# Products and operand sums in another order, slabs in pairs, and weight sums one stage sooner in a chunk attention, Fourier mixing and MLP kernel on Trainium2

## The chip, the cores and the metric

The kernel runs on one core of one Trainium2 chip. The metric is the time of one execution on the device in microseconds; the kernel before took 1138.69 us (median of three runs, 1135.14 to 1141.55). A profile of one further execution is at hand for the kernel before. Engine names in the profile: PE is TensorE (PEld its weight loads), DVE is VectorE, ACT is ScalarE, POOL is GpSimd, SP is SyncE, which issues most DMAs.

## What is computed

Eight batches of 576 tokens, 8 heads of 64 elements. Attention runs inside chunks of 64 tokens; its output x (576 x 512 per batch) is mixed by the real part of a two-dimensional Fourier transform, then a normalised MLP with a hidden width of 2048 is added. Everything is float32.

```python
scores = scale * np.matmul(q_c, k_c.transpose(0, 1, 2, 4, 3))     # per chunk of 64 tokens
attn = softmax(scores); x = np.matmul(attn, v_c)                  # then (B, S, H*D)
mixed = np.real(np.fft.fft(np.fft.fft(x, axis=1), axis=2))
u = x + mixed
un = (u - mean(u)) / np.sqrt(var(u) + 1e-06)
out = u + np.maximum(un @ w_ch1, 0.0) @ w_ch2                     # w_ch1 512x2048, w_ch2 2048x512
```

The weights arrive as float64 and are rounded to float32 in the kernel.

## The kernel before

*Tiles and stages.* A tile is 128 tokens. A stage of the MLP handles a group of four tiles (512 tokens); there are nine stages: one for each batch and a last one for the four tiles of left-over tokens. Within a group the tiles are LO, HI, LO, HI: an HI tile holds its features reversed. Each stage has an up half (un @ w_ch1, with ReLU, into the hidden tile `h1`) and a down half (`h1` @ w_ch2, plus u, stored to DRAM). While TensorE works on stage g, the attention and the mixing of batch g + 1 are woven in between the MLP's steps: the main loop takes one step of `mlp(g)`, then as many steps of `side(b)` (attention, then `fourier`) as are due, then the work on the weights. The instructions of each engine, SP's DMA queue included, run in the order in which this loop writes them (`manual_schedule`); waits between engines are set by the buffers that they share. SP issues the loads of q, k and v (`load`, `load_v`, L236 and L259), the stores of the result (`store`, L1013 and L1022, some of them on ACT) and the slabs of weights.

*Stages 0 and 1* are plain products with both weights resident in SBUF: `wa` holds w_ch1 (four rows k of 2048 columns), `wb` holds w_ch2 (sixteen rows m of 512). `up_first`, `up_plain` (L1130) and `down_plain` (L1147) take 16 steps for each half, so that stage 1 runs from t = 32 (`begin[1]`) to t = 64 (`begin[2]`).

*Stages 2 to 8* use fewer products on half-size blocks. `up_halves` takes seven products where a plain two by two split has eight: each product is four matmuls (two row blocks r, two kk) of 128x128 by 128x256, and the sums that it needs are taken by VectorE (L1199, L1201, L1203, L1207, L1210) and ACT. `down_halves` takes 26 products of four matmuls each (L1238): `h1` is seen as 4 x 4 blocks a_ij (tile i, quarter j of the hidden width), w_ch2 as 4 x 2 blocks b_ij. `PRODUCTS` lists, for each product, the left operand (an a block or one of the sums y0 to y3 in `yall`), the right operand (a b block or a made sum s..), the half bank of PSUM that it goes to (four banks; a capital letter is the upper half), and the output blocks that it is added to. A half bank that comes again is not cleared: the new product is added to what stands there. VectorE adds or subtracts a half bank to the output (L1248), which must be done before TensorE writes to that half bank again. The a blocks are overwritten in place by POOL's operand sums (`SUMS`, L1098): those named "early" during the up half, the others after the product whose name they carry.

*Weights for these stages.* During stage 1, `keep1` makes the four sums of w_ch1's blocks on POOL (into `yall`) and stores seven slabs for each of four groups to DRAM (`s1`); it has five steps a group. `keep_raw` stores the raw blocks of w_ch2, and `keep_made` makes their 23 sums (`MADE`, L1066: every third on POOL, the others on VectorE), in slots that lie in `wa` and `yall`, and stores the 18 that are needed (`s2`). In the loop, two steps of `keep1` and one raw block are done at each t from `begin[1]` on; the sums, two at each t, begin after `begin[1] + KF` (t = 49); when the last is made (t = 60), ten slabs of `s1` are fetched; at t = 64 six slabs of `s2`.

*Slabs.* In stages 2 to 8, `fetch(1)` brings the next slab of 256 KB of `s1` into one of ten slots in `wa` after each up product (L1078), and `fetch(2)` the next slab of 512 KB of `s2` into one of six slots in `wb` after each down product (L1081). A fetch waits until TensorE is done with the slab that it overwrites.

*Mixing* ends, for each of two LO, HI pairs of tiles, with two VectorE operations on the products (L834, L835), the sum x + mixed for the LO tile on VectorE and for the HI tile on POOL (both L841), and the statistics of both on VectorE (L688, L689). It falls into the first products of a down half.

The lines of the kernel before, as the profile names them:

Of the kernel before, what the change touches and what calls it, by code (L numbers as in the profile page):

```python
# [16 lines left out]
def kernel(  # L17
# [87 lines left out]
    s1 = dram.tile([HF // 2, NO, 128, 2 * 2 * 128], FP32, name="s1")  # L105
    NS1, NS2, Z1, Z2 = 10, 6, 2 * 2 * 128, 4 * HM
    slab1 = [wa[:, i * Z1:(i + 1) * Z1].rearrange("p (k r f) -> p k r f", r=2, k=2) for i in range(NS1)]
    slab2 = [wb[:, i * Z2:(i + 1) * Z2].rearrange("p (m e) -> p m e", m=4) for i in range(NS2)]
# [6 lines left out]
        ("2", "a41", "b11", "c", "+41"), ("13", "a44", "b42", "b", "+42"), ("8", "y0", "s8", "d", "+12"),  # L115
        ("21", "y3", "s21", "c", "+31+32+42"), ("0", "y1", "s0", "d", "+11+21"), ("16", "a22", "b22", "f", "-22"),
        ("19", "a23", "s19", "d", "+22"), ("15", "a44", "s15", "b", "+41"), ("10", "a31", "s10", "f", "+32"),
        ("3", "y1", "s3", "b", "-21-22"), ("11", "y3", "b32", "f", "+42"), ("5", "a22", "b21", "C", "+31"),
        ("24", "a21", "s24", "B", "-32-42"), ("1", "a31", "s1", "D", "-21+41"), ("17", "a13", "s17", "F", "+11"),
        ("4", "a24", "s4", "C", "-21"), ("22", "a41", "s22", "B", "-21"), ("25", "a32", "s25", "D", "-32"),  # L120
        ("12", "a34", "s12", "F", "+12"), ("20", "a43", "b31", "C", "+41"), ("7", "a11", "s7", "B", ""),
        ("6", "a14", "s6", "D", ""), ("18", "y2", "s18", "F", "-32"), ("9", "a12", "b21", "B", "-11"),
        ("14", "y0", "b22", "D", "+12"), ("23", "a33", "s23", "F", "-31"),
    )
    SUMS = {
        "early": "y0=a11-a13 a11=a11-a21 y1=y0-a21 y2=a31-a41 a31=a33-a31 y3=y2-a33",
        "": "a24=a23+a24", "2": "a41=a22+a42 a22=a21-a22 a21=a41-a21", "13": "a44=a24+a44 a31=a21+a31",
        "21": "y3=y3+a43", "0": "y1=a44-y1 y1=y1-a23 y0=a12-y0", "16": "a22=a32-a34 a32=a42-a32",
        "10": "a31=a42-a22 a13=a13+a14 a24=a24+a31 a14=a14+a34 a34=a13+a34 y2=a34+y2",
        "11": "a43=a44+a43 a12=a41-a12 a12=a12+a13 y0=y0-a32",  # L130
    }
    RAW = ("b11", "b42", "b22", "b32", "b21", "b31")
    MADE = (
        "u=b41-b31 0", "s15=u-b42 1", "s7=u-b11 2", "s8=b12+b22 3", "s0=u-s8 4", "t=b32-b42 5", "s19=u+t 5",
        "s3=b31-b41 6", "s10=b11-b12 0", "s21=s10-b32 1", "s24=s10-b22 2", "v=b32-b31 3", "s23=v-s10 3",
        "w=b22-b21 4", "s22=w-s10 5", "s4=b42-b41 6", "s25=w+s4 4", "s1=b21-s4 2", "s17=b21+b41 0",
        "h=b12+b32 1", "s12=h-s17 3", "s6=b42-h 5", "s18=-h 1",
    )
    SLABS = RAW + tuple(name.split("=")[0] for name in MADE if name[0] == "s")
    NR2 = len(PRODUCTS)  # L140
    s2 = dram.tile([len(SLABS), 128, Z2], FP32, name="s2")
# [39 lines left out]
    def kind(n):  # L181
        return tiles[n][0]
# [595 lines left out]
    def fourier(b):  # L778
# [59 lines left out]
        def added(y, n):  # L838
            x, w = xt(n), DM + (kind(n) == HI)
            eng = nc.gpsimd if kind(n) == HI else nc.vector  # L840
            eng.tensor_tensor(out=x[:, 0:w], in0=y[:, 0:w], in1=x[:, 0:w], op=ALU.add)  # L841
# [183 lines left out]
    def keep1(i):  # L1025
# [11 lines left out]
        to = s1.rearrange("a o p (k x) -> p a o k x", k=2)[:, 2 * f:2 * f + 2]  # L1037
        for o, a in enumerate((a11, o2, o1, o3, a12, o4, a22)):
            nc.sync.dma_start(out=to[:, :, o, kk], in_=a.rearrange("p (a x) -> p a x", a=2))
# [6 lines left out]

    def keep_raw(name):
        to = s2[SLABS.index(name)].rearrange("p (m e) -> p m e", m=4)
        nc.sync.dma_start(out=to, in_=block_b(name))

    at_slot = {}

    def keep_made(i):

        text, slot = MADE[i].split()
        space = wa[:, 0:5 * Z2] if int(slot) < 5 else yall.rearrange("p a b -> p (a b)")
        j = int(slot) % 5
        to = space[:, j * Z2:(j + 1) * Z2].rearrange("p (m e) -> p m e", m=4)
        if "=-" in text:
            name, a = text.split("=-")  # L1060
            nc.vector.tensor_scalar(to, at_slot[a], -1.0, None, ALU.mult)
        else:
            name, a, b, op = parsed(text)
            eng = nc.gpsimd if i % 3 == 2 else nc.vector
            in0, in1 = (block_b(x) if x[0] == "b" else at_slot[x] for x in (a, b))
            eng.tensor_tensor(out=to, in0=in0, in1=in1, op=op)  # L1066
        at_slot[name] = to
        if name in SLABS:
            nc.sync.dma_start(out=s2[SLABS.index(name)], in_=to.rearrange("p m e -> p (m e)"))

# [3 lines left out]
    def fetch(which):  # L1074
        i = n_slab[which]
        if which == 1 and i < HF // 2 * NO * (NG - first_of[1]):
            pair, o = divmod(i % (HF // 2 * NO), NO)
            nc.sync.dma_start(out=slab1[i % NS1].rearrange("p k r f -> p (k r f)"), in_=s1[pair, UP[o]])  # L1078
        elif which == 2 and i < NR2 * (NG - first_of[2]):
            slab = SLABS.index(PRODUCTS[i % NR2][2])  # L1080
            nc.sync.dma_start(out=slab2[i % NS2].rearrange("p m e -> p (m e)"), in_=s2[slab])  # L1081
        n_slab[which] = i + 1
# [93 lines left out]
    def up_halves(g):  # L1176
# [3 lines left out]
        for pair in range(HF // 2):  # L1180
            pas, pbs = {}, {}
            for turn_, o in enumerate(UP):
                w = slab1[((g - first_of[1]) * HF // 2 * NO + pair * NO + turn_) % NS1]
# [28 lines left out]
                fetch(1)  # L1212
                if pair == HF // 4 and turn_ > 0:
                    sums(h1, SUMS["early"].split()[turn_ - 1:turn_])
                if turn_ in (1, 3, 5, 6):
                    yield h1

    def down_halves(g, h1):
        banks, begun = {}, set()
        left = [sum(p[4].count(f"{i + 1}{j + 1}") for p in PRODUCTS for j in range(2)) for i in range(G)]  # L1220
        sums(h1, SUMS[""].split())
        for o, (name, a, _, bank, reads) in enumerate(PRODUCTS):
            w, lhs = slab2[((g - first_of[2]) * NR2 + o) % NS2], block_a(h1, a)
# [28 lines left out]
            sums(h1, SUMS.get(name, "").split())  # L1252
            fetch(2)
            if o % 2 == 0:
                continue
            if g + 1 < NG:
                for j in range(G):
                    if k == 3 + 2 * j:
                        normed(g + 1, j)
                    if k == 5 + 2 * j and j >= 2:  # L1260
                        combined(g + 1, j - 2)
# [8 lines left out]
    with tc.manual_schedule():  # L1270
# [73 lines left out]
        for g in range(NG):  # L1344
            for _ in mlp(g):
# [23 lines left out]
                if t >= begin[1]:  # L1369
                    for _ in range(2):  # L1370
                        next(conv1, None)
# [3 lines left out]
                if t > begin[1] + KF and n_made < len(MADE):  # L1375
                    for _ in range(2):
                        if n_made < len(MADE):
                            keep_made(n_made)
                            n_made += 1
                    if n_made == len(MADE):  # L1380
                        for _ in range(NS1):
                            fetch(1)
                if t == begin[2]:
# [51 lines left out]
```

## Time and profile before

| | |
|---|---|
| runs | 1138.69 us median (1135.14, 1138.69, 1141.55) |
| profiled execution | 1134.59 us, span 1132.7 us from its first instruction to its last |
| granted TensorE clock | 0.977 mean |
| HBM | 203.5 MB read, 29.4 MB written, 206 GB/s over the span |
| SP's DMA queue | 163372 packets, 229.54 MB |
| slabs of `s2` (wb<-s) | 182 DMAs of 512 KB |
| slabs of `s1` (wa<-s) | 196 DMAs of 256 KB |
| start of stages 1, 2 and 3 on TensorE | 190, 318 and 450 us |
| start of stages 4 to 8 | 573, 700, 824, 940 and 1036 us |

How to read it: times in the timeline count from the span's start. A line such as `657.00 1.97 PE L1238 MATMUL dn<-wb,yall ... x8 [0.79 <-issue]` says when a run of instructions began, how long it lasted, the engine, the source line, what it writes and reads, how many there were, and in brackets how long the engine had been idle before and what ended that wait. A matmul in float32 appears as two rows, so that one product of four matmuls is eight rows. The waits view adds the same brackets up: who waited for whom, microseconds in total, how often, the longest.

### The profile page before, as it was taken

The page shows a single profiled execution, that of the slowest core. Times are in us where ns is not written, and L with a number is a line of the kernel's source. Part 1 is how long each engine was busy: PE and PEld are TensorE (multiplying, and loading weights), DVE is VectorE, ACT ScalarE, POOL GpSimd, SP SyncE. Part 2 cuts the span into 40 slices and gives each one's busy share as a digit, 9 for nine tenths or more (in the row PEclk, how much of TensorE's full clock was granted, in tenths as well). Part 3 has the DMA queues.
Part 4 walks back from the last instruction along what each step waited for, and adds up shares of the span by engine and source line. Part 5 has one row for each costly group of instructions (what it writes and reads, how often), then busy time and mean ns, then how long its engine had stood idle before and what let it go on. Part 6 is the DMA issues. An engine that isn't in the chain of part 4 may idle for free.

```text
span 1132.7 us, 19622 instructions
## 1 busy us (share of the span) xinstructions
PE 1061.9 (94%) x7210; PEld 812.1 (72%) x7210; DVE 585.1 (52%) x1275; ACT 306.5 (27%) x716; POOL 440.0 (39%) x518
## 2 busy tenths in 40 slices
PE   8999989999996989799989989898989999999998
PEld 6645444444565877687878877687878788888886
DVE  4899873235854355454545465444653543333332
ACT  4697553211121310232122311222022302201210
POOL 4311011365414580076406560078325640380272
PEclk9999999999998999999998999999999999999999
DMA  7767512885468868796778668876865676587456
GB/s 167 233 194 203 139 43 64 287 257 197 184 178 258 251 199 273 199 242 198 228 219 227 206 211 249 221 201 195 271 230 141 195 244 224 161 286 262 125 200 209
DMA packets 167117, 234.20 MB, mean 207 GB/s; under 512 B 70092, under 2 KB 106956, under 8 KB 167022
## 3 DMA queue, kind: packets, MB, share of 16 engines
q1 hardware_dynamic: 163372, 229.54, 66.7%
q10 hardware_dynamic: 3330, 2.76, 0.9%
q8 instruction: 58, 0.95, 0.4%
q0 software_dynamic: 320, 0.66, 0.2%
q14 instruction: 37, 0.30, 0.1%
HBM read 203.53 MB, written 29.36 MB: 206 GB/s over the span
## 4 chain that ended last, share of the span: by engine, by line
PE 70%; DMA 10%; DVE 7%; POOL 4%; ACT 3%; SPq 3%; issue 2%; POOLq 0%; DVEq 0%; ACTq 0%
PE dn L1238 24%; PE pa L1193 15%; PE pb L1193 11%; PE dn L1147 6%; PE up L1130 5%; DMA wb<-s 3%; PE pt L383 2%; DMA k<-in_k_dram 2%; POOL xall L841 2%; DMA xall<-in_moe_w_ch_dram 2%; PE z L705 1%; SPq L249 1%; PE xp L484 1%; PE sc L434 1%; POOL h L1098 1%
## 5 line engine op out<-in xcount | busy, mean ns | idle before, releaser
L1238 PE MATMUL dn<-wb,h 128*128 128x256 f32 x1064 | 240.9, 380 | 0.7 <-DMA wb<-s 0.7
L1238 PEld LDWEIGHTS dn<-wb,h 128*128 128x128 f32 x1064 | 198.9, 190 | 26.6 <-DVE wb L1248 1.1
L1098 POOL TENSOR_TENSOR h<-h 128x512 f32<-128x512 f32 x126 | 161.2, 1293 | 91.0 <-ACT h L1211 70.2
L1193 PE MATMUL pa<-unT,wa 128*128 128x256 f32 x672 | 163.2, 386 | 9.2 <-DVE wa L1201 9.2
L1193 PEld LDWEIGHTS pa<-unT,wa 128*128 128x128 f32 x672 | 127.9, 192 | 28.4 <-DVE wa L1201 10.0
L1248 DVE TENSOR_TENSOR wb<-wb,dn 128x256 f32<-128x256 f32 x154 | 61.6, 417 | 129.5 <-PE dn L1238 129.5
L1238 PE MATMUL dn<-wb,yall 128*128 128x256 f32 x392 | 101.3, 411 | 19.4 <-DVE wb L1248 11.9
L1147 PE MATMUL dn<-wb,h 128*128 128x512 f32 x256 | 114.6, 597 | 0.0
L1193 PE MATMUL pb<-wa 128*128 128x256 f32 x448 | 107.2, 382 | 0.0
L1238 PEld LDWEIGHTS dn<-wb,yall 128*128 128x128 f32 x392 | 78.8, 205 | 35.6 <-DVE wb L1248 13.9
L1193 PEld LDWEIGHTS pb<-wa 128*128 128x128 f32 x448 | 84.6, 191 | 12.4 <-DVE o L1160 0.7
L1147 PEld LDWEIGHTS dn<-wb,h 128*128 128x128 f32 x256 | 46.9, 190 | 51.7 <-issue 50.5
L541 POOL COPY xall<-xall 1x512 f32<-1x512 f32 x28 | 17.8, 635 | 147.0 <-DVE xall L501 119.5
L1193 PE MATMUL pb<-unT,wa 128*128 128x256 f32 x224 | 54.8, 388 | 12.7 <-DMA wa<-s 12.7
L1205 ACT ACTIVATE h<-pa 128x256 f32<-128x256 f32 x56 | 21.5, 384 | 155.3 <-PE pa L1193 155.3
L1210 DVE TENSOR_TENSOR h<-pb,wa 128x256 f32<-128x256 f32 x56 | 23.8, 425 | 73.9 <-PE pb L1193 73.9
L1193 PEld LDWEIGHTS pb<-unT,wa 128*128 128x128 f32 x224 | 43.7, 196 | 20.0 <-issue 13.9
L1130 PE MATMUL up<-unT,wa 128*128 128x512 f32 x128 | 56.6, 595 | 0.0
L1193 PE MATMUL pa<-wa 128*128 128x256 f32 x224 | 56.3, 396 | 0.0
L1199 DVE TENSOR_TENSOR wa<-pb,wa 128x256 f32<-128x256 f32 x56 | 23.4, 423 | 57.3 <-ACT wa L1198 57.3
L1098 POOL TENSOR_TENSOR yall<-h 128x512 f32<-128x512 f32 x14 | 17.8, 1270 | 86.5 <-ACT h L1211 86.2
L512 POOL COPY xall<-xall 128x1 f32<-128x1 f32 x15 | 2.8, 186 | 124.9 <-DVE xall L501 107.7
(258 smaller groups left out, 1602.6 us busy)
## 6 DMA issues: line engine op xcount, KB each, us to landing
wb<-s SPq DMA_DIRECT2D x182, 512.0 KB
wa<-s SPq DMA_DIRECT2D x196, 256.0 KB
xall<-in_moe_w_ch_dram SPq DMA_DIRECT2D x22, 512.0 KB
q<-in_q_dram SPq DMA_DIRECT2D x96, 112.0 KB
k<-in_k_dram SPq DMA_DIRECT2D x96, 112.0 KB
v<-in_v_dram SPq DMA_DIRECT2D x124, 64.0 KB
s<-wa SPq DMA_DIRECT2D x13, 512.0 KB
yall<-in_moe_w_ch_dram SPq DMA_DIRECT2D x10, 512.0 KB
```

Source lines behind the costliest of these rows:

```text
L383: nc.tensor.transpose(pt[:, j, :], src(j), ident)
L541: nc.gpsimd.tensor_copy(to, from_)
L841: eng.tensor_tensor(out=x[:, 0:w], in0=y[:, 0:w], in1=x[:, 0:w], op=ALU.add)
L1098: nc.gpsimd.tensor_tensor(out=out_, in0=a, in1=b, op=op)
L1130: nc.tensor.matmul(out=up, lhsT=w1[:, kk, m * 128:(m + 1) * 128], rhs=unT[:, kk], start=(kk == 0), stop=(kk == KD - 1),)
L1147: nc.tensor.matmul(out=dn, lhsT=h1[:, m, s * 128:(s + 1) * 128], rhs=w2[:, m, :], start=(m == 0), stop=(m == KF - 1),)
L1193: nc.tensor.matmul(out=dst, lhsT=w[:, kk, r], rhs=rhs[o][:, kk], start=(o in (0, 1) and kk == 0), stop=(kk == 1), skip_group_check=True,)
L1199: nc.vector.tensor_tensor(out=b, in0=pbs[r][:, 0], in1=a, op=ALU.add)
L1205: nc.scalar.activation(out=h1[:, m, lo], in_=dst, func=ACTF.Relu)
L1210: nc.vector.tensor_tensor(out=h1[:, HF + m, lo], in0=dst, in1=b, op=ALU.add)
L1238: nc.tensor.matmul(out=dst, lhsT=lhs[:, m], rhs=w[:, m], start=(fresh and not half and m == 0), stop=(m == 3), skip_group_check=True,)
L1248: nc.vector.tensor_tensor(out=to, in0=base, in1=dst, op=ALU.add if sign_ == "+" else ALU.subtract)
```

## The change

The 26 products stand in another order, go to other half banks, and carry the operand sums that follow them; no sum is named apart any more but the early ones. Each slab of `s1` and `s2` in DRAM now holds two consecutive ones (`s1`: four of a pair of rows, the last half full; `s2`: 13 of 1 MB, in the order of the products, so that a raw block that is used twice is stored twice), there are five and three slots, and a fetch comes once for two products. `keep1` takes three steps at each t, the sums of w_ch2 begin after `begin[1] + KF // 2` (t = 41) with one or two at each t and six slots in place of seven, and the store of a sum is written two sums later (`behind`). The first fetches are at `begin[2] - 6` (t = 58) and `begin[2] - 3` (t = 61). Mixing's sum for an HI tile is on VectorE for all batches but batch 1.

```diff
-    NS1, NS2, Z1, Z2 = 10, 6, 2 * 2 * 128, 4 * HM
+    s1 = dram.tile([HF // 2, 4, 128, 2 * 2 * 2 * 128], FP32, name="s1")
+    NS1, NS2, Z1, Z2 = 5, 3, 2 * 2 * 2 * 128, 2 * 4 * HM
...
     PRODUCTS = (
-        ("2", "a41", "b11", "c", "+41"), ("13", "a44", "b42", "b", "+42"), ("8", "y0", "s8", "d", "+12"),
-        ("21", "y3", "s21", "c", "+31+32+42"), ("0", "y1", "s0", "d", "+11+21"), ("16", "a22", "b22", "f", "-22"),
-        ("19", "a23", "s19", "d", "+22"), ("15", "a44", "s15", "b", "+41"), ("10", "a31", "s10", "f", "+32"),
-        ("3", "y1", "s3", "b", "-21-22"), ("11", "y3", "b32", "f", "+42"), ("5", "a22", "b21", "C", "+31"),
...
+        ("a41", "b11", "c", "+41", "a13=a13+a14"),
+        ("a44", "b42", "b", "+42", "a41=a22+a42"),
+        ("y0", "s8", "d", "+12", "a22=a21-a22"),
+        ("a13", "s17", "a", "+11", ""),
+        ("y3", "s21", "c", "+31+32+42", "a21=a41-a21"),
+        ("a22", "b22", "C", "-22", "a24=a23+a24"),
+        ("a21", "s24", "D", "-32-42", "y0=a12-y0 a44=a24+a44 a31=a21+a31"),
+        ("y1", "s0", "d", "+11+21", "a22=a32-a34"),
+        ("a44", "s15", "b", "+41", "a32=a42-a32"),
+        ("a31", "s10", "C", "+32", "a31=a42-a22 a24=a24+a31"),
+        ("a41", "s22", "D", "-21", ""),
+        ("a23", "s19", "d", "+22", "a14=a14+a34 a34=a13+a34"),
+        ("a31", "s1", "A", "-21+41", ""),
+        ("a22", "b21", "B", "+31", "y1=a44-y1 y1=y1-a23"),
+        ("a11", "s7", "D", "", "a12=a41-a12 y2=a34+y2"),
+        ("a34", "s12", "a", "+12", ""),
+        ("a32", "s25", "A", "-32", ""),
+        ("y1", "s3", "b", "-21-22", ""),
+        ("a24", "s4", "B", "-21", "y0=y0-a32 y3=y3+a43"),
+        ("y2", "s18", "a", "-32", "a43=a44+a43"),
+        ("a14", "s6", "A", "", ""),
+        ("y3", "b32", "C", "+42", ""),
+        ("a43", "b31", "B", "+41", "a12=a12+a13"),
+        ("a12", "b21", "D", "-11", ""),
+        ("a33", "s23", "a", "-31", ""),
+        ("y0", "b22", "A", "+12", ""),
     )
...
-            eng = nc.gpsimd if kind(n) == HI else nc.vector
+            eng = nc.gpsimd if kind(n) == HI and b == 1 else nc.vector
...
+    def kept(name):
+        return [s2[i // 2, :, i % 2 * 4 * HM:(i % 2 + 1) * 4 * HM] for i, p in enumerate(PRODUCTS) if p[1] == name]
...
+        while behind and (i >= len(MADE) or behind[0][0] <= i - 2):
+            _, old, from_ = behind.pop(0)
+            for dst in kept(old):
+                nc.sync.dma_start(out=dst, in_=from_.rearrange("p m e -> p (m e)"))
+        if i < len(MADE):
+            behind.append((i, name, to))
...
-                fetch(1)
                 if pair == HF // 4 and turn_ > 0:
...
                 if turn_ in (1, 3, 5, 6):
+                    fetch(1)
                     yield h1
...
-            sums(h1, SUMS.get(name, "").split())
-            fetch(2)
+            sums(h1, then.split())
             if o % 2 == 0:
                 continue
+            fetch(2)
...
                 if t >= begin[1]:
-                    for _ in range(2):
+                    for _ in range(3):
                         next(conv1, None)
...
-                if t > begin[1] + KF and n_made < len(MADE):
-                    for _ in range(2):
-                        if n_made < len(MADE):
+                if t > begin[1] + KF // 2:
+                    for _ in range(1 + t % 2):
+                        if n_made <= len(MADE):
                             keep_made(n_made)
                             n_made += 1
-                    if n_made == len(MADE):
-                        for _ in range(NS1):
-                            fetch(1)
-                if t == begin[2]:
+                if t == begin[2] - 6:
+                    for _ in range(NS1):
+                        fetch(1)
+                if t == begin[2] - 3:
                     for _ in range(NS2):
                         fetch(2)
```

## The prediction

> **What bounds the kernel now.** I read the busy shares first, then TensorE's waits from 318 us on (where the stages with 7 and 26 products begin), then the rows around single waits.
>
> ```profile
> span 1132.7 us, 19622 instructions
> PE 1061.9 (94%) x7210; PEld 812.1 (72%) x7210; DVE 585.1 (52%) x1275; ACT 306.5 (27%) x716; POOL 440.0 (39%) x518
> ```
>
> TensorE is busy 94% of the span, so the change, which keeps every product, can only win idle time of TensorE: 1132.7 - 1061.9 = 70.8 us. Busy times by stretch (columns: length, busy us and count of PE, PEld, DVE, ACT, POOL, granted clock, DMA share, GB/s) say where it lies:
>
> ```profile
> 190.00:318.00 128.00, 127.48 (x735) 62.05 (x733) 64.66 (x97) 22.32 (x54) 63.21 (x66) 1.00 0.67 225
> 318.00:940.00 622.00, 571.09 (x4266) 485.71 (x4267) 313.21 (x708) 134.80 (x354) 274.19 (x332) 0.96 0.74 220
> 987.00:1035.60 48.60, 48.60 (x235) 42.80 (x234) 19.01 (x45) 1.98 (x4) 27.23 (x22) 1.00 0.84 283
> ```
>
> Stage 1 (190 to 318) has 0.5 us of idle, stages 2 to 6 (318 to 940) have 622.00 - 571.09 = 50.9, a down half without a batch beside it (987 to 1035.6) none, though DMA moves 283 GB/s there. All that can be won in the 26-product stages is thus in these 50.9 us. TensorE's waits in that part (us in total, times, longest):
>
> ```profile
> PE pb L1193 <- DMA wa<-s: 12.7, 3, 10.6
> PE dn L1238 <- DVE wb L1248: 11.9, 5, 2.4
> PE pa L1193 <- DVE wa L1201: 9.2, 2, 4.8
> PE sc L434 <- DVE kT L402: 7.7, 3, 4.1
> PE dn L1238 <- DMA wb<-s: 5.2, 3, 2.6
> PE dn L1238 <- issue: 2.8, 3, 1.2
> ```
>
> The first row's 10.6 is one wait, 337.70 to 348.27: the first up half runs out of slabs, because its eleventh one is issued at 340.63, behind eight stores of stage 1, a q load and the six slabs of the down half. Rows two and six belong together; in stage 4 they look like this (start, us, idle before):
>
> ```profile
> 657.00 1.97 PE L1238 MATMUL dn<-wb,yall 128*128 128x256 f32 x8 [0.79 <-issue]
> 661.35 1.14 PE L1238 MATMUL dn<-wb,yall 128*128 128x256 f32 x3 [2.38 <-DVE wb L1248]
> ...
> 654.04 1.27 POOL L841 TENSOR_TENSOR xall<-y,xall 128x513 f32<-128x513 f32 x1
> 658.34 1.70 POOL L841 TENSOR_TENSOR xall<-y,xall 128x513 f32<-128x513 f32 x1 [3.02 <-DVE y L835]
> ...
> 655.35 0.69 DVE L688 BATCH_NORM_STATS2 bst<-xall 128x6 f32<-128x512 f32 x1 [1.46 <-POOL xall L841]
> 660.90 1.05 DVE L1248 TENSOR_TENSOR wb<-wb,dn 128x256 f32<-128x256 f32 x3
> ```
>
> VectorE stands on POOL's mixing sum (1.46 us, POOL still having SUMS to do); three drains L1248 pile up behind it, and TensorE, whose product 10 writes the half bank of product 8, waits.
>
> **The change, part by part.** (a) *Order of the products.* One product is 8 rows, 1.73 us (32 rows in 6.91 in the chain). Before, bank d is written by products 2, 4, 6 and f by 5, 8, 10, so the drain between has one or two products, 1.7 to 3.5 us. After, no half bank comes again before the fourth product (c 0, 4; d 2, 7, 11; b 1, 8, 17; C 5, 9, 21; D 6, 10, 14, 23; A 12, 16, 20, 25): three products, 5.2 us. VectorE's block for a mixing tile is two L834/L835 (0.42 each), two sums (0.69), two statistics (0.69 + 0.18): 4.0 us, plus a drain 0.42: 4.4. That fits into 5.2. Rows two and six, 11.9 + 2.8 = **14.7 us, go**.
>
> (b) *Operand sums.* Still 21 on POOL a stage, 1.27 us each, 27 us in a half of 45 or more. The tightest are a31, issued when product 9 ends and read by 12 (3.5 us for 1.3), and a12 after product 22, read by 23, which in stages 2 and 4 now stands behind a qT copy (L404) that waits for VectorE's transpose: at 688.34 before, with product 22 at 687.1 if its slab is there; 688.5 + 1.3 = 689.8 against a product 23 at 689.2: 0.6 twice, **+1 us** (0 to 3).
>
> (c) *Mixing's sums on VectorE*: for batches 2 to 7, 12 sums. POOL's row is 1.27 to 1.70, VectorE's 0.69, so VectorE gets 12 x 0.69 = 8 us, inside (a)'s block. But VectorE's sums from SBUF stretch beside POOL: L1066 1.21 alone, 2.53 at 288.41 beside POOL's L1066; L841 once 1.61 for 0.69. Two of 1.61 make the block 6.3 us against 5.2: 1.1 us on the path if both are hit; 16 of 18 L841 rows were not stretched. I take **+1** in all, bounds 0 and 8 (seven tiles hit).
> The Trainium skill ("SBUF — State Buffer", section "Who interferes with whom") says more: a VectorE instruction with two SBUF inputs and a reading GpSimd instruction exclude each other, so the later one blocks fully. By that each moved sum could wait one POOL row, 12 x 1.27 = 15 us of VectorE; all of it on the path would make the time 1134.
>
> (d) *Slabs in pairs.* The bytes are the same (13.6 MB a down half), the issues half. Before, the refill of a slot has 5 products, 8.6 us; the DMA records show the last packet 2.84 us after an undisturbed issue (639.12): 5.8 us to spare. After, a pair's refill comes when its second product ends and is read four products on, 6.9 us; its 256 packets of 8 KB are one more 1.27 us (8 packets of 4 KB an engine at 159 ns), 4.1: 2.8 to spare. SP's issues are late by more than that in the second part of a half:
>
> ```profile
> 674.34 1.65 SPq L1081 DMA_DIRECT2D wb<-s  x2
> 676.49 2.71 SPq L236 DMA_DIRECT2D k<-in_k_dram  x4
> 684.07 0.81 SPq L1022 DMA_DIRECT2D out_dram<-wb  x2
> 684.99 1.34 SPq L1081 DMA_DIRECT2D wb<-s  x3
> ```
>
> Product 17 ended at 678.4, its refill went out at 685.45, 7.0 late, behind a k load and the store of row 2. Per stage the worst odd product is late by 7.6, 6.4, 7.0, 5.3 (stages 2 to 5); with 2.8 to spare that is 4.8 + 3.6 + 4.2 + 2.5 = 15.1 of waits for the 5.2 there are: +9.9. Against it: row 2 is now complete at product 18, not 16, so that refill passes ahead of the store, and 13 issues for 26 leave SP less to wait for. Bounds -5.2 and +9.9; **I take 0**, nearest to the row of today's waits. In the up halves slot 10 is needed one product sooner (1.03 and 1.16 now waited), but a wait for VectorE (4.83, 4.39) follows at once and ends where it ended: 0.
>
> (e) *Weight sums sooner.* First gain: the up half's five slab pairs are issued six steps before stage 2 and the down half's three pairs three steps before, both now ahead of the stage's eight stores and the next q and k loads; the wait at 337.70 goes, **-10.6** (at worst half: they share DMA with 18 made slabs, still being stored until 306.85 before, and some 15 us earlier now). Price: two more raw slabs to DRAM (1 MB, off the path) and stage 1, which had no idle, gets 15 VectorE sums of 1.2 to 2.5 us and 8 on POOL (2.35) amid attention. On VectorE the first two stand between a qT and a kT transpose, and the second writes the row of w1 which the last `keep1` group stores. POOL resumed 3.7 us after a group's yall store was issued (208.87 to 212.59), works 5.1, and SP adds about 1: 10 us a group. First group issued at 204.9, the fourth 30 us later, landed 3.7 after, then 1.2 (sum) and 1.1 (kT): 240.9. TensorE's score step needs that kT at 236.0: **+5 us** (0 if a group takes 8 us, 15 if 13). The batch's later steps move with TensorE, and the sums that stood around the norms (288 to 305) are gone there.
>
> Rows three and four (9.2 + 7.7) hang on q and k loads that come late after a down half; neither moves: 0 (-9 to +6).
>
> Sum: -14.7 - 10.6 + 1 + 1 + 0 + 5 = -18.3. Profiled span 1132.7 gives 1114.4; its run took 1134.6, 4.1 under the median 1138.7 of the runs. I predict by the median: 1138.7 - 18.3 = **1120**.
>
> **The rivals.** *Everything late goes too:* with fewer issues in front, q and k land in time: a further -5.2 and half of 16.9: 1138.7 - 18.3 - 13.7 = 1107. For it: SP's queue is what is late in all of these rows; against: the loads' own bytes remain, and DMA is at 1.0 of its share around the end of stage 4. *Stage 1 gives it back:* `keep1` at three steps makes SP stand at its stores, and k, then TensorE, wait 15: 1138.7 - 25.3 + 15 + 2 = 1130. For it: POOL already waited 14.88 for a yall store. Against: DMA is at 0.67 there. *Slower, late pairs:* 1 MB in the same queue doubles what each late issue waits for; latenesses of 15.2, 12.8, 14.0 and 10.6 less 2.8 are 41.4 of waits, +36.2: 1138.7 - 18.3 + 36.2 = 1157. It decides from +24 on, latenesses about 1.6 times today's. For it: room of 2.8 instead of 5.8 us; against: the store that causes the two worst moves behind the refill, and the halves without a batch ran at 283 GB/s with no wait. *It doesn't do what it says* I give nothing: the order of instructions in the built program is as the diff reads.
>
> **How the numbers follow.** Forecast 0.55 (1108 to 1131), all-late-goes 0.20, stage 1 0.13, late pairs 0.12. The range 1098 to 1143 takes the low bounds of (d), rows three and four, and (e)'s 0 at one end, and the upper bounds of (c), (d) and (e) without all meeting at the other. 0.5% (5.7 us) is what this measurement can tell from no change. Faster: 0.55 + 0.20 + 0.04 of stage 1; same 0.09; slower 0.12.
>
> **What would show it.** (a) and (c): no wait of TensorE for L1248 in the down halves, POOL's L841 left at batch 1 only. (e): no wait for wa slabs near 340, and a new one at a score step near 240. (d): waits for wb slabs near 5 us in sum, in the second part of stages 2 to 5. Wrong if wb waits pass 30 us, if stage 1 idles over 15, or if a drain still holds a bank.

## The result, and the profile after

The changed kernel takes 1177.29 us (median of four runs, 1172.05 to 1180.22); the kernel before, run beside it, 1136.91 (1132.15 to 1141.55). The ratio is 1.035, 95% interval 1.0289 to 1.0411: slower, and outside the range of the prediction (1098 to 1143). The profiled execution took 1172.05 us, its span 1170.3 against 1132.7. The page of the changed kernel begins:

```profile
span 1170.3 us, 19148 instructions
PE 1070.2 (91%) x7210; PEld 812.0 (69%) x7210; DVE 590.0 (50%) x1287; ACT 307.2 (26%) x716; POOL 419.7 (36%) x506
```

TensorE has the same 7210 rows; its idle time rose from 70.8 to 100.1 us, VectorE's work hardly at all. Its waits in the changed kernel (us in total, times, longest):

```profile
PE dn L1261 <- DVE wb L1271: 46.4, 37, 3.5
PE sc L444 <- DVE kT L412: 16.0, 3, 6.4
PE pa L1217 <- DMA wa<-s: 15.3, 5, 6.4
...
PE dn L1261 <- POOL h L1122: 1.8, 2, 0.9
...
PE dn L1261 <- DMA wb<-s: 0.3, 1, 0.3
```

The first row is the one that was to go: 11.9 us in five waits became 46.4 in 37. The last was 5.2 us. Busy times by stretch, columns as before (stages 2 to 6, then the down half of stage 7, where no batch runs beside the MLP):

```profile
327.50:961.40 633.90, 571.32 (x4261) 484.07 (x4261) 319.76 (x717) 135.53 (x354) 258.80 (x322) 0.97 0.66 209
1011.00:1064.20 53.20, 48.56 (x226) 40.74 (x225) 19.19 (x44) 1.89 (x4) 27.31 (x22) 1.00 0.73 253
```

A down half without any attention or mixing had no idle time before and took 46.65 us; now it idles 4.64 of 53.13. So the new waits need no mixing and no late slab. The timeline of the changed kernel in that half (start, us, idle before) shows the first two:

```profile
1017.92 1.89 PE L1261 MATMUL dn<-wb,yall 128*128 128x256 f32 x8
1021.08 3.69 PE L1261 MATMUL dn<-wb,h 128*128 128x256 f32 x16 [1.27 <-DVE wb L1271]
1025.62 2.00 PE L1261 MATMUL dn<-wb,yall 128*128 128x256 f32 x8 [0.85 <-DVE wb L1271]
...
1019.85 0.75 DVE L1271 TENSOR_TENSOR wb<-xall,dn 128x256 f32<-128x256 f32 x2 [1.31 <-PE dn L1261]
1020.52 0.41 DVE L1271 TENSOR_TENSOR wb<-wb,dn 128x256 f32<-128x256 f32 x1
```

Product 4 goes to half bank c and ends near 1019.8. VectorE drains it three times (+31, +32, +42), until 1020.93. Product 5 starts at 1021.08. It writes C, the *other* half of the same bank, for the first time in this stage; nothing of C was being read. In the kernel both halves are slices of one PSUM buffer (`dn`), and the wait is for the whole buffer. Product 7 (d) waits in the same way for the two drains of product 6 (D).

Sorted by product over the seven stages, the 46.4 us are: product 5, 13.7; 7, 18.1; 11, 0.5; 16, 2.6; 18, 5.0; 20, 1.5; 25, 4.9. These seven products, and no others, directly follow the one that writes the other half of their bank (c C, D d, D d, a A, b B, a A, a A). In the order before, lower halves fill products 0 to 10 and upper ones 11 to 25, and the closest such pair (b in product 9, B in product 12) is three products apart.

Lengths of the same stretches of TensorE's work in the profiled executions, as differences to the kernel before in us (their sum is the difference of the spans), tell where each kernel won and lost. "Downs" are the down halves of stages 2 to 8, "ups" the up halves of 3 to 8.

| kernel | median us | ratio to before, 95% | stages 0 and 1 | up of 2 | downs | ups |
|---|---|---|---|---|---|---|
| after | 1177.29 | 1.0289 to 1.0411 | +9.6 | -9.7 | +34.4 | +3.3 |
| e1_banks | 1123.33 | 0.9829 to 0.994 | +9.6 | -9.8 | -17.4 | +8.2 |
| e2_old_order | 1147.41 | 1.0051 to 1.0192 | +11.5 | -9.8 | +24.1 | -13.6 |
| e3_only_order | 1173.44 | 1.0266 to 1.04 | -0.5 | 0.0 | +30.8 | +3.9 |
| e4_mix_pool | 1174.87 | 1.0226 to 1.0397 | +11.2 | -9.6 | +35.5 | +7.8 |
| e5_banks_two | 1126.83 | 0.9894 to 0.9946 | +12.9 | -9.7 | -18.0 | +7.2 |
| e6_banks_pool | 1131.53 | 0.9951 to 1.0007 | +9.9 | -9.2 | -9.3 | +7.9 |
| e7_up_singles | 1128.42 | 0.9898 to 0.9954 | +9.4 | -10.1 | -14.2 | +10.2 |
| e8_sums_later | 1122.87 | 0.9841 to 0.9914 | +8.1 | -8.9 | -16.3 | +4.3 |
| e9_good_order_only | 1137.86 | 0.999 to 1.0027 | -1.7 | +0.1 | -11.4 | +16.3 |
| e10_stage1_both | 1125.5 | 0.9899 to 0.9943 | +11.5 | -8.9 | -12.6 | +4.0 |
| e11_stage1_old | 1123.07 | 0.9872 to 0.9932 | -0.5 | +2.7 | -15.1 | +2.7 |
| e12_down_singles | 1133.63 | 0.9969 to 1.0021 | +9.1 | -6.9 | -19.5 | +16.0 |

The runs of the kernel before beside them had medians of 1135.54 (e1 to e4), 1135.88 (e5, e7 to e9) and 1134.94 (e6, e10 to e12).

### The profile page after: what moved, and what is told of

The parts are those of the page before. It is cut to its first block, busy times and chain, and to the rows that moved or that the text cites. A ratio compares the mean times of both kernels' runs of the same rounds, so it can differ in the third digit from the quotient of the medians.

```text
span 1170.3 us, 19148 instructions
## 1 busy us (share of the span) xinstructions
PE 1070.2 (91%) x7210; PEld 812.0 (69%) x7210; DVE 590.0 (50%) x1287; ACT 307.2 (26%) x716; POOL 419.7 (36%) x506
## 4 chain that ended last, share of the span: by engine, by line
PE 66%; DMA 11%; DVE 11%; issue 3%; ACT 3%; POOL 3%; SPq 2%; DVEq 0%; ACTq 0%; POOLq 0%
PE dn L1261 24%; PE pa L1217 15%; PE pb L1217 10%; PE dn L1171 6%; DMA wa<-s 4%; DVE wb L1271 3%; PE mix L834 2%; DMA k<-in_k_dram 2%; PE pt L393 2%; POOL yall L1045 2%; PE up L1134 1%; DMA xall<-in_moe_w_ch_dram 1%; PE up L1154 1%; PE z L715 1%; SPq L259 1%
## 5 line engine op out<-in xcount | busy, mean ns | idle before, releaser
L1261 PE MATMUL dn<-wb,h 128*128 128x256 f32 x1064 | 249.3, 385 | 26.2 <-DVE wb L1271 23.4
L1217 PE MATMUL pa<-unT,wa 128*128 128x256 f32 x672 | 160.0, 381 | 0.0
L1261 PE MATMUL dn<-wb,yall 128*128 128x256 f32 x392 | 97.2, 392 | 23.0 <-DVE wb L1271 23.0
L1261 PEld LDWEIGHTS dn<-wb,yall 128*128 128x128 f32 x392 | 74.0, 194 | 38.1 <-DVE wb L1271 28.6
L1217 PEld LDWEIGHTS pb<-wa 128*128 128x128 f32 x448 | 84.1, 190 | 11.9 <-DVE o L1184 0.7
L1217 PE MATMUL pa<-wa 128*128 128x256 f32 x224 | 59.8, 415 | 15.3 <-DMA wa<-s 15.3
L551 POOL COPY xall<-xall 1x512 f32<-1x512 f32 x28 | 18.7, 669 | 137.5 <-DVE xall L511 110.6
L1217 PEld LDWEIGHTS pa<-wa 128*128 128x128 f32 x224 | 45.5, 208 | 24.0 <-issue 14.5
L1154 PE MATMUL up<-unT,wa 128*128 128x512 f32 x128 | 58.7, 613 | 0.0
L1271 DVE TENSOR_TENSOR wb<-xall,dn 128x256 f32<-128x256 f32 x56 | 22.8, 417 | 54.6 <-PE dn L1261 54.6
L1134 PE MATMUL up<-unT,wa 128*128 128x512 f32 x108 | 49.4, 598 | 0.0
```

The lines of the kernel that those rows point to most:

```text
L1134: nc.tensor.matmul(out=up, lhsT=w1[:, kk, m * 128:(m + 1) * 128], rhs=unT[:, kk], start=(kk == 0), stop=(kk == KD - 1), skip_group_check=True,
L1154: nc.tensor.matmul(out=up, lhsT=w1[:, kk, m * 128:(m + 1) * 128], rhs=unT[:, kk], start=(kk == 0), stop=(kk == KD - 1),)
L1217: nc.tensor.matmul(out=dst, lhsT=w[:, kk, r], rhs=rhs[o][:, kk], start=(o in (0, 1) and kk == 0), stop=(kk == 1), skip_group_check=True,)
L1261: nc.tensor.matmul(out=dst, lhsT=lhs[:, m], rhs=w[:, m], start=(fresh and not half and m == 0), stop=(m == 3), skip_group_check=True,)
L1271: nc.vector.tensor_tensor(out=to, in0=base, in1=dst, op=ALU.add if sign_ == "+" else ALU.subtract)
```

## The experiments: what the lost time hangs on

**e1_banks.** Only the letters of the upper half banks change: C and A are exchanged, and D and B. Order, operand sums, slabs and drains stay; no product now directly follows the one in its bank's other half.

```diff
-        ("a22", "b22", "C", "-22", "a24=a23+a24"),
-        ("a21", "s24", "D", "-32-42", "y0=a12-y0 a44=a24+a44 a31=a21+a31"),
+        ("a22", "b22", "A", "-22", "a24=a23+a24"),
+        ("a21", "s24", "B", "-32-42", "y0=a12-y0 a44=a24+a44 a31=a21+a31"),
...
-        ("a11", "s7", "D", "", "a12=a41-a12 y2=a34+y2"),
+        ("a11", "s7", "B", "", "a12=a41-a12 y2=a34+y2"),
```

> The changed kernel with its eight half banks paired otherwise (lower a, b, c, d now share a bank with the products that wrote C, D, A and B), so that no two products that follow each other directly write halves of one bank; order, sums, slabs and all else as changed. Theory 1 (TensorE waits for the drain of the other half of the same bank, not only of its own half): the waits for the drain L1271 fall from 46.4 us to 15 or less, what is left lies in the mixing of stages 2 to 6, and the time is about 1137 (1128 to 1148). Theory 2 (the drains come late because VectorE carries the mixing sums beside POOL): the letters do not matter, 1171 to 1183. Theory 3 (slab pairs and earlier weight sums cost the time): 1171 to 1183 too.

Measured: 1123.33 us, ratio 0.9884: theory 1, and even below its window. TensorE's waits in e1_banks:

```profile
PE pa L1217 <- DMA wa<-s: 18.7, 5, 8.0
PE sc L444 <- DVE kT L412: 17.5, 3, 6.5
PE dn L1261 <- DVE wb L1271: 7.1, 5, 1.4
PE dn L1261 <- issue: 3.3, 5, 0.8
```

Fourteen changed letters are worth 54 us: the drain's waits fall from 46.4 to 7.1, one of 1.41 in each of stages 2 to 6, at product 10. Stage 7 is back at 46.65. The last row is one wait at product 8 in each of the same stages. Stage 4 in e1_banks:

```profile
651.23 3.69 PE L1261 MATMUL dn<-wb,h 128*128 128x256 f32 x16 [0.55 <-issue]
656.33 1.99 PE L1261 MATMUL dn<-wb,h 128*128 128x256 f32 x8 [1.41 <-DVE wb L1271]
...
650.41 1.05 DVE L1271 TENSOR_TENSOR wb<-wb,dn 128x256 f32<-128x256 f32 x3
655.89 0.72 DVE L1271 TENSOR_TENSOR wb<-wb,dn 128x256 f32<-128x256 f32 x2
```

These waits are for mates too, now with one product between. Product 10 (B) starts at 656.33, when the first drain of the last row, of product 8 (b), ends at 656.28; its own half, last written by product 6, had been drained by 651.12. Product 8 (b) starts at 651.23, just after that drain of product 6 (B); the view names no releaser there, but in all five stages it starts 0.10 to 0.11 us after product 6's last drain.

**e3_only_order.** The kernel before with nothing but the new order, banks and operand sums.

```diff
-        ("2", "a41", "b11", "c", "+41"), ("13", "a44", "b42", "b", "+42"), ("8", "y0", "s8", "d", "+12"),
+        ("p0", "a41", "b11", "c", "+41"),
+        ("p1", "a44", "b42", "b", "+42"),
+        ("p2", "y0", "s8", "d", "+12"),
+        ("p3", "a13", "s17", "a", "+11"),
+        ("p4", "y3", "s21", "c", "+31+32+42"),
+        ("p5", "a22", "b22", "C", "-22"),
...
```

> The kernel before with the products, half banks and operand sums in the changed order and nothing else of the change. Theory 1: some 5 us of drain waits and 1.5 us of restarts come into each of the seven down halves, +45, less what the old order waited: 1165 to 1185. Theory 2: POOL still makes the mixing sums, so 1125 to 1145. Theory 3: 1125 to 1145.

Measured: 1173.44 us, ratio 1.0333: theory 1. TensorE's waits for the drain in e3_only_order:

```profile
PE dn L1267 <- DVE wb L1277: 44.9, 37, 3.2
```

The order alone makes the kernel as slow as the whole change.

**e2_old_order.** The changed kernel with the old order, banks and operand sums: what the rest of the change does.

```diff
-        ("a41", "b11", "c", "+41", "a13=a13+a14"),
-        ("a44", "b42", "b", "+42", "a41=a22+a42"),
+        ("a41", "b11", "c", "+41", "a41=a22+a42 a22=a21-a22 a21=a41-a21"),
+        ("a44", "b42", "b", "+42", "a44=a24+a44 a31=a21+a31"),
...
+        sums(h1, "a24=a23+a24".split())
         for o, (a, _, bank, reads, then) in enumerate(PRODUCTS):
```

> The changed kernel with the products, half banks and operand sums in the order of before; slab pairs, earlier weight sums and mixing's sums on VectorE as changed. Theory 1: no product shares a bank with the one just before, so the down halves lose their new waits; with the won first slab wait (-9.7) and the stage 1 loss (+9.5) the time is 1125 to 1142. Theory 2: VectorE's mixing sums stay, so 1160 to 1180. Theory 3: 1165 to 1180.

Measured: 1147.41 us, ratio 1.0121: slower than theory 1 said, faster than the others. The rest is not free where the old order stands. TensorE's waits for late slabs in e2_old_order, and the mixing's sum for an HI tile (busy us, mean ns of one, idle before):

```profile
PE dn L1262 <- DMA wb<-s: 15.1, 5, 4.0
```

```profile
L851 DVE TENSOR_TENSOR xall<-y,xall 128x513 f32<-128x513 f32 x12 | 18.9, 1574 | 0.0
```

The same row in the changed kernel:

```profile
L851 DVE TENSOR_TENSOR xall<-y,xall 128x513 f32<-128x513 f32 x12 | 8.2, 686 | 0.0
```

With the old operand sums POOL works through a row of them just when VectorE adds; the moved sums are stretched by 0.9 us on average, and the drains' waits are 22.4 us (longest 4.8). With the new ones POOL mostly waits for a product there (3.46 us before 662.50 in stage 4), or is the one held up (two sums in 2.97 us at 656.06, for 2.5). So the moved sums are cheap beside the new order of POOL's work and dear beside the old one.

**e4_mix_pool.** The changed kernel with the mixing's sums on POOL again.

```diff
-            eng = nc.gpsimd if kind(n) == HI and b == 1 else nc.vector
+            eng = nc.gpsimd if kind(n) == HI else nc.vector
```

> The changed kernel with mixing's sum for the HI tiles back on POOL for all batches. Theory 1: only the waits of product 7 in stages 2 to 6 (3.3 us) and of product 5 move a little, 1168 to 1186. Theory 2: 1140 to 1160, and the waits for L1271 fall by more than 20 us.

Measured: 1174.87 us, ratio 1.0312; 44.9 us in 37 waits for the drain. Theory 1; VectorE's new work isn't what lost the time.

## The experiments: what the parts are worth once the banks are right

**e9_good_order_only.** The kernel before with e1's order and banks: e3's edit with e1's letters.

```diff
-        ("p5", "a22", "b22", "C", "-22"),
-        ("p6", "a21", "s24", "D", "-32-42"),
+        ("p5", "a22", "b22", "A", "-22"),
+        ("p6", "a21", "s24", "B", "-32-42"),
...
```

> The kernel before with the products, operand sums and re-paired banks of e1_banks alone: slabs single, weight sums at their old place, the mixing's sums on GpSimd. Theory 1 (the new order is worth the 14.7 us of the prediction's first term once no half follows its mate, and e1's gain in the seven down halves, 17.4 us, is its own): the drain's waits fall below 9 us, time 1116 to 1126. Theory 2 (most of e1's gain comes from the earlier weight sums and the mixing's sums on VectorE, and the order alone brings little): 1128 to 1137.

Measured: 1137.86 us, ratio 1.0009: no gain, a miss for theory 1 (the drain's waits are 9.7 us, not below 9) and 0.9 us above theory 2's window. The downs win 11.4 us and the ups lose 16.3. In stage 4 the score step waits 8.38 us for kT instead of 4.13. SP's queue around the start of stage 4 (near 572 us here) in e9_good_order_only:

```profile
579.99 2.81 SPq L1042 DMA_DIRECT2D out_dram<-wb  x2
582.90 2.92 SPq L1110 DMA_DIRECT2D wb<-s  x1
585.91 3.68 SPq L265 DMA_DIRECT2D k<-in_k_dram  x4
```

The same in e1_banks, with slabs in pairs:

```profile
572.01 4.18 SPq L1023 DMA_DIRECT2D out_dram<-wb  x4
576.29 2.35 SPq L1105 DMA_DIRECT2D wb<-s  x1
578.73 2.40 SPq L246 DMA_DIRECT2D k<-in_k_dram  x4
```

k goes out behind the stores of the finished rows and the last slab fetch: at 582.54 in the kernel before, 585.91 in e9, 578.73 in e1. The score step that needs it starts 13.0, 12.9 and 13.5 us later (595.53, 598.83, 592.23). So what sets this step is when SP lets k go, not when TensorE is done with the products; after a down half that ends sooner it only waits longer. In e2, whose down halves end later, the waits for kT in stages 4 and 6 all but go (0.35 us and none, 4.13 and 3.43 before), and the up halves are 13.6 us shorter. SP's queue is what must get shorter, and halving the fetches does that (e12 below). Why k goes out 3.4 us later in e9 than before, no run isolates.

**e12_down_singles** (slabs of `s2` single again) and **e7_up_singles** (slabs of `s1` single again), both on e1_banks:

```diff
-    NS1, NS2, Z1, Z2 = 5, 3, 2 * 2 * 2 * 128, 2 * 4 * HM
+    NS1, NS2, Z1, Z2 = 5, 6, 2 * 2 * 2 * 128, 4 * HM
...
-    s2 = dram.tile([NR2 // 2, 128, Z2], FP32, name="s2")
+    s2 = dram.tile([NR2, 128, Z2], FP32, name="s2")
...
+            fetch(2)
             if o % 2 == 0:
                 continue
-            fetch(2)
```

> e1_banks with the down slabs single as before the change (six of 512 KB, one fetched after each product); the up slabs stay in pairs. Theory 1 (the pairs relieve SP at the end of a down half, where the last slab's fetch stands ahead of k's loads): kT comes 2 to 4 us later in stages 4 and 6, the up halves of stages 3 to 6 together 6 to 14 us longer than in e1, time 1128 to 1138. Theory 2 (the slabs' size doesn't count once the order has no stalls): 1120 to 1126.

```diff
-    s1 = dram.tile([HF // 2, 4, 128, 2 * 2 * 2 * 128], FP32, name="s1")
-    NS1, NS2, Z1, Z2 = 5, 3, 2 * 2 * 2 * 128, 2 * 4 * HM
+    s1 = dram.tile([HF // 2, NO, 128, 2 * 2 * 128], FP32, name="s1")
+    NS1, NS2, Z1, Z2 = 10, 3, 2 * 2 * 128, 2 * 4 * HM
...
+                fetch(1)
                 if pair == HF // 4 and turn_ > 0:
...
                 if turn_ in (1, 3, 5, 6):
-                    fetch(1)
                     yield h1
```

> e1_banks with the up slabs single as before the change (ten of 256 KB, one fetched after each product); the down slabs stay in pairs. Theory 1 (the 18.7 us of waits for wa in the up halves come from the pairs: one product, about 1.1 us, less of lead and twice the bytes to land): they fall to 6 to 12 us, time 1113 to 1119. Theory 2 (they come from what stands ahead on SP's queue, the v loads above all, whatever the slab's size): they stay at 15 to 20 us, time 1121 to 1126.

e12: 1133.63 us, ratio 0.9995; theory 1. The downs are no longer than e1's, the ups 7.8 us longer (16.0 against 8.2) and the up of stage 2 another 2.9, with waits for kT of 6.87 and 8.17 in stages 4 and 6 (e1: 5.29, 5.68) and 22.9 us of waits for `wa` slabs (e1: 18.7). Pairs in the down halves are worth some 10 us, in the halves *after* them. e7: 1128.42 us; both theories missed. The waits for wa did fall, from 18.7 to 5.9 us, but 8.2 us of waits for VectorE's sums and longer ones elsewhere came in their place, and the time did not improve. Its interval overlaps e1's, so a loss of some 5 us is likely but not settled.

**e6_banks_pool.** e1_banks with e4's edit.

> e1_banks with the mixing's sums of one kind on GpSimd again, as before the change. The order alone (e9) brought nothing, because the up halves took back what the down halves won; e1 keeps it. Theory 1 (it is the pairs that keep it, as they halve the fetches ahead of q, k and v on SP): time within 4 us of e1_banks, 1120 to 1127. Theory 2 (it is the mixing's sums on VectorE, which take work out of GpSimd's stretch of operand sums): the waits for POOL's sums come back in stages 2 to 6 (1.2 us in each), time 1129 to 1136.

Measured: 1131.53 us, ratio 0.9979; theory 2. TensorE's waits in e6_banks_pool:

```profile
PE dn L1261 <- DVE wb L1271: 9.8, 6, 1.9
PE dn L1261 <- POOL h L1122: 8.1, 7, 1.4
```

POOL's waits are back (1.8 us in e1), and the downs lose 8.1 us (-9.3 against -17.4). Moving the mixing's sums to VectorE is worth 8 us, where the prediction gave it a cost of 1; in the changed kernel itself e4 shows no difference. So it takes the pairs and the moved sums together to keep what the order wins; either one undone brings the kernel back to the time before.

**e11_stage1_old**, **e5_banks_two**, **e8_sums_later** and **e10_stage1_both** go after the weight sums in stage 1, all on e1_banks. e11 undoes them:

```diff
                 if t >= begin[1]:
-                    for _ in range(3):
+                    for _ in range(2):
                         next(conv1, None)
...
-                if t > begin[1] + KF // 2:
-                    for _ in range(1 + t % 2):
+                if t > begin[1] + KF:
+                    for _ in range(2):
...
-                if t == begin[2] - 6:
+                if t == begin[2] - 3:
```

> e1_banks with stage 1 as before the change: up weights' sums at two steps per turn, down weights' sums begun at the seventeenth turn, first slabs fetched three turns later. Theory 1 (what the earlier weight sums save in stage 2, 9.8 us, they give back in stage 1, 9.6 us): stages 0 and 1 317 to 319 us, the first wait for a slab is back with 8 to 11 us, time 1120 to 1127, within 4 us of e1_banks. Theory 2 (the earlier sums are worth the 10.6 us of the prediction): 1130 to 1136.

Measured: 1123.07 us, theory 1: stages 0 and 1 are back at 317.37 us, the first wait for a slab is back with 11.55, and the time is e1's. What the earlier sums save they cost, as far as the times can tell: the two ratios (0.9902, 0.9884) together leave room for some 5 us either way. VectorE in stage 1 of the changed kernel shows where:

```profile
234.74 1.10 DVE L412 STREAM_TRANSPOSE qT<-q 128x512 f32<-128x512 f32 x1 [14.90 <-DMA q<-in_q_dram]
235.69 1.58 DVE L1084 TENSOR_TENSOR wa<-wb 128x1024 f32<-128x1024 f32 x1
239.53 2.39 DVE L1084 TENSOR_TENSOR wa<-wa,wb 128x1024 f32<-128x1024 f32 x1 [2.25 <-DMA s<-wa]
241.84 1.07 DVE L412 STREAM_TRANSPOSE kT<-k 128x512 f32<-128x512 f32 x1
```

kT comes 10 us later than before (231.93). Two causes: q was loaded late (qT at 228.75 before), and a weight sum that waits for a store stands ahead of kT. e5 takes only two steps of `keep1` at a time again, e8 begins the weight sums three turns later:

```diff
-                    for _ in range(3):
+                    for _ in range(2):
                         next(conv1, None)
```

> The changed kernel with the halves of the banks paired anew (as in e1_banks, 1123.3 us), and the up weights' operand sums again at two steps per turn instead of three. Theory 1 (the 6.53 us wait for kT at 236.78 in stage 1 is made of two things: q and k of that step are issued 6 us later because SP stands behind stores of the third and fourth batch of sums, and VectorE's weight sum, waiting 2.90 us for a store, stands between qT and kT): the batch moves behind q and k, qT comes near 229 as in the kernel before, the wait falls below 1.5 us, stages 0 and 1 become 5 to 8 us shorter, time 1115 to 1119. Theory 2 (the weight sums on VectorE alone make it): the wait stays above 4 us, time 1121 to 1126.

```diff
-                if t > begin[1] + KF // 2:
-                    for _ in range(1 + t % 2):
+                if t > begin[1] + KF // 2 + 3:
+                    for _ in range(2):
```

> e1_banks with the down weights' sums begun three turns later in stage 1 (two per turn, so that they end at the same turn); the up weights' sums keep their three steps. Theory 1 (both causes): kT follows qT at once, near 236, and the wait at 236.78 falls to 1 to 2.5 us; time 1117 to 1121. Theory 2 (weight sums alone): wait below 1 us, time 1115 to 1119. Theory 3 (only the late q and k loads count): wait stays above 4 us, time 1121 to 1126.

e5: 1126.83 us with a wait of 11.85: not theory 1, and above theory 2's time. qT is back at 229.31, k is issued at 226.83 as before, but the fourth group's stores now come later, and the two weight sums wait longer for them. VectorE in e5_banks_two:

```profile
235.73 1.22 DVE L1084 TENSOR_TENSOR wa<-wb 128x1024 f32<-128x1024 f32 x1 [5.31 <-DMA s<-wa]
242.51 3.02 DVE L1084 TENSOR_TENSOR wa<-wa,wb 128x1024 f32<-128x1024 f32 x1 [5.56 <-DMA s<-wa]
245.46 1.07 DVE L412 STREAM_TRANSPOSE kT<-k 128x512 f32<-128x512 f32 x1
```

e8: 1122.87 us with a wait of 4.49: theory 3, the late loads alone. kT follows k's landing at once, at 240.47, but k was issued at 233.86, behind a group's stores. So e5 speaks for the weight sums and e8 for the loads: each edit removes one cause and leaves the other.

> e1_banks with both edits of stage 1 at once: the up weights' operand sums at two steps per turn (e5) and the down weights' sums begun three turns later (e8). Theory 1 (two causes in a row: with two steps q and k land in time, but a weight sum that waits for a store stands ahead of kT; with later sums kT is free, but q and k land late): the wait for kT near 236 all but goes (below 1 us), stages 0 and 1 come to 317 to 321 us instead of 327.5, time 1113 to 1119. Theory 2 (each is enough by itself to leave what the other would mend, something third holds the step): the wait stays above 3 us, time 1120 to 1126.

e10 (both edits): 1125.5 us, a miss. The wait at 236 is gone (kT at 234.43), as theory 1 said, but stages 0 and 1 are not shorter (+11.5). The mixing's own steps come later in stage 1, and now wait: 2.39 us at 265.93 for POOL's pm, and 3.89 at 287.84, where VectorE's zs sums begin at 288.75, behind weight sums that wait for POOL's in turn. At all four paces tried (e1, e5, e8, e10) the earlier sums cost stages 0 and 1 between 8 and 13 us; a place for them that costs nothing was not found.

## Why the prediction was wrong, by its own steps

(a) *Order: -14.7 predicted; the changed kernel's down halves became 34.4 us longer.* The failed step is "no half bank comes again before the fourth product", and so a room of three products, 5.2 us. The sentence is true of half banks, and I took the half as the unit that a drain holds (as the description of the kernel above does). In this program the unit is the bank: seven of the 26 products follow their mate (the product in the other half of their bank) with no product between, so the room was 0, not 5.2 us, and 11.9 us of waits became 46.4 instead of none. The timeline (stage 7), e3 (the order alone is slow) and e1 (letters alone mend it) show it. The rivals missed it too: "it doesn't do what it says" got nothing because the order is as the diff reads; the waits that follow from it were not worked out. "If a drain still holds a bank" did name the sign. The Trainium skill has the rule ("PSUM — Partial Sum Buffer", section "PSUM bank collisions raise a hardware error"): two engines must not touch the same bank and the same quadrant of partitions at once, not even in different columns. The waits here agree with a program built to that rule; the error itself occurs in no run here, and no run shows what the chip would do without the wait. By that page the prediction should have counted mates.

With the mates apart the order alone shortens the down halves by 11.4 us (e9), not 14.7, and the time not at all; the -17.4 of e1 hold the pairs and the moved sums as well. Of the two rows that were to go, 14.7 us, e1 still has 10.4, at products 8 and 10, which have one product between themselves and their mates: a room of 1.73 us against VectorE's 4.4. Idle time in the down halves fell by 8.1 us in e1; the other 9.3 are about what the slow products after the waits had cost (9.4, last section). So the change could win more than idle time, against the prediction's opening step: a product at half clock counts as busy, and the busy time is 1061.9 us before and 1053.4 in e1.

(b) *Operand sums: +1.* About right: product 23 waits for POOL in stages 2 and 4, 0.92 and 0.93 us (predicted 0.6 twice).

(c) *Mixing's sums: +1.* Wrong in sign. They are worth -8 (e6), since (a) had booked all waits around the mixing on the order; without the move POOL has 8.1 us of them, 6.4 at product 8, which reads one of POOL's sums. The stretch beside POOL that the Trainium skill's rule ("SBUF — State Buffer", section "Who interferes with whom") speaks of is real, and large in e2 (1574 ns for 686), but only where POOL reads at that moment and came first; in the changed kernel none of the twelve moved sums met a sum of POOL's.

(d) *Pairs: 0, bounds -5.2 and +9.9.* Between: in the changed kernel waits for wb fall from 5.2 to 0.3. With the old order they are 15.1 us in five waits (e2). That this is the sum of the latenesses that were worked out is luck: stages 2 to 5 wait 2.52, 3.97, 2.95 and 3.66, where 4.8, 3.6, 4.2 and 2.5 were said, and the fifth wait, 2.0, is in stage 8. (A pair is 128 packets of 8 KB, a median of 309 ns each for the 159 of 4 KB, not 256 packets; the 1.27 us taken for it hardly change.) What was not seen is that the pairs pay elsewhere: some 10 us, through SP's queue ahead of k and of the up halves' slabs (e12). "Up halves 0" was off by little in total: +3.3 over six halves, of which 2.3 in stages 7 and 8, where new waits of 1.02 and 0.81 appear.

(e) *Weight sums: -10.6 + 5.* The gain was right (-9.7). The cost was right in place and cause (score step ready at 236.56, kT done at 242.9; predicted 236.0 and 240.9) and too small: the wait is 6.4, another of 1.5 comes at 216, and the whole of stages 0 and 1 grows by 9.6. Net about nothing (e11), not -5.6, though the interval does not quite shut that out. The rival "stage 1 gives it back" was right in kind: SP stands at the stores of `keep1`'s sums ahead of q and k; its 15 us were too many.

The slower rival (late pairs, 1157) had the direction and the wrong mechanism: waits for wb are 0.3 us.

## What to carry to other kernels

Where half banks serve as accumulators, count the distance between products by bank, mates included, and hold it against the longest block of the engine that drains; the listing of letters shows it before any run. In e1 one product between mates, 1.73 us, was still too little while VectorE had its block of 4.4. A gain in one part of a stage is kept only if what the next part waits for also comes sooner: ask which queue issues it, and what stands ahead. Undo the parts of a change one by one on the mended version as well as on the broken one; here the order alone brings nothing (e9), the rest alone costs 1.2% (e2), and together they bring 1.2% (e1_banks, which beats both kernels).

## What the runs showed of the hardware

A wait of TensorE can cost more than half as much again after it has ended. In stage 4 of the kernel before, after the wait of 2.38 us at 658.97 (columns as in the stretches above; the third from the end is the granted clock):

```profile
662.00:665.00 3.00, 3.00 (x10) 2.35 (x9) 0.34 (x1) 0.00 (x0) 2.94 (x3) 0.50 0.05 19
```

In e1_banks, after the wait of 1.41 us in the same place:

```profile
658.00:661.00 3.00, 3.00 (x18) 2.64 (x17) 0.89 (x3) 1.12 (x2) 2.92 (x3) 1.00 0.33 137
```

Ten rows of matmuls in the time of eighteen. In the down halves before, six of the seven waits between 1.96 and 2.56 us were followed by a product 1.2 to 1.7 us slow (3.07 to 3.52 us from its start to the next row, against 1.83 after the waits of 1.41 in e1; 9.4 us in all, five of the six after a wait of 2.38); of the five waits of 1.85 in e9 one was, of the five of 1.41 in e1 none. So the five waits of 2.38 cost some 20 us, not the 11.9 of the waits view. It does not follow every wait: in the changed kernel five of eight waits from 2.4 to 3.5 us were followed by a product 0.4 to 1.4 us slow.

The clock records of all fourteen profiles say the same. From 190 us on the granted clock falls to 0.50 117 times; 14 of these, one in each profile, lie in the last 4 us of the span, and each of the other 103 begins during a wait of TensorE of 0.5 us or more, or within 3.4 us after one. By the length of the wait: none of 243 from 0.5 to 1.45 us, 3 of 26 up to 1.95, 38 of 61 up to 4, 62 of 63 above.

Apart from that, each wait costs an estimated 0.3 us to start again: the down half of stage 7, at a clock of 1.00 throughout, is 6.48 us longer in the changed kernel for six waits and 4.64 us of idle time. The Trainium skill ("TensorE: Matmul & The Clock Gate", section "HAM oscillation — how this bites in real kernels") gives idle gaps over about 3.4 us as what to avoid; here shorter ones were enough.
